# Gate and up tiles beside attention: three groups of eight pieces instead of two of twelve

## The chip, the core and the metric

The kernel runs on one core of a Trainium2 chip. The core has five engines, each with its own queue of instructions that it takes in order: PE (TensorE: matmuls, and their weight loads, PEld), DVE (VectorE), ACT (ScalarE), POOL (GpSimd) and SP (SyncE, which here only issues DMAs; POOL and ACT issue some too). They wait for each other through semaphores. The metric is the device time of one execution in microseconds (us).

## The reference

One transformer block with conditioning, in float32: S = 2048 rows, D = 512 columns, 32 heads of 16, a feed-forward part of F = 1792 columns. Six vectors (shift, scale and gate for each half) come from the condition `c`.

```python
mod = (_silu(c) @ w_mod).reshape(c.shape[0], 6, 1, -1)
sa, ca, ga, sb, cb, gb = (mod[:, i] for i in range(6))
h = _layernorm(x) * (1 + ca) + sa
qkv = split_heads(h @ wqkv)                    # 32 heads of 16
p = softmax(q @ k.T * 16 ** -0.5)              # whole rows, 2048 x 2048 per head
x = x + ga * (merge_heads(p @ v) @ wo)
h = _layernorm(x) * (1 + cb) + sb
x = x + gb * ((silu(h @ w_gate) * (h @ w_up)) @ w_down)
```

## The kernel before

**Tiling.** The 2048 rows are four chunks of 512 (`NC`, `CW`), the heads eight groups of four (`NG`). A *unit* is one chunk of queries with one group of heads, 32 units in all; chunk 0 is units 0 to 7, and so on. A unit has 16 *steps*, one for each 128 keys, so there are 512 steps. A step has four *slots* (`pair_of`, one for each head of the group): a score matmul (L569) that ACT turns into exponentials (L571), and one maximum matmul (L521) whose row maxima DVE takes (L523). The maxima are for a unit ahead: step i takes those of step i + 20, since the exponentials of a unit need all its row maxima first. When a unit's maxima are done, they are written as two extra rows into its query tile `qop`: by `max_rows` through PE, ACT and two DMAs of SP (L540, `qop<-mr`), or by `max_turned` through DVE and eight DMAs of SP (L560, `qop<-turned`). The score matmuls of that unit read those rows. P times V (L584, `pv_step`) follows a few steps behind, in halves.

**Two kinds of stretches.** `plain(steps)` runs steps with attention alone, in windows of three slots; scores take turns in three PSUM banks (4, 5, 6), maxima in four (0, 1, 2, 3). `filled(places, work)` runs eight slots (two steps) and after slot r takes `places[r]` pieces of other work; then the halves of P times V stand in a block. Scores then have two banks (4, 5), maxima three (0, 1, 2), and the other work sums into banks 3 and 6 (`FBANKS`). A *piece* is one step of `accumulate`: two matmuls of 64 rows, side by side on the two halves of the array. A gate and up tile (128 columns of F, `gate_up`) is 24 pieces: 12 with one assignment of halves to banks (`ph` 0), 12 with the other. A pair of `down` is 12 pieces, 6 and 6. Between the two assignments `down` calls `read_both`: ACT reads one element of each bank, so that PE's second half waits until the first is through. `gate_up` had no such read; its two assignments fell into two groups.

**Who is scheduled where.** For chunks 0, 1 and 2 the output projection and the feed-forward part run beside the attention of later units: from `STARTS[ci]` (steps 147, 275, 403) on come 8 filled steps for the output projection, 12 plain ones, then the chunk's jobs: 14 tiles of gate and up (f = 0 to 13) and 14 of down. Chunk 2 has `REST` = 24 further plain steps ahead of its jobs, and leaves `KEEP` = 7 jobs to the end. What remains up to the next chunk's start is plain: `plain(STARTS[ci] - done // 4)`. Chunk 3 runs after attention.

**What goes by the count of steps.** Work that is tied to attention is put off with `at(i, f)` and comes after step i, whatever runs beside it. When the last unit of a chunk closes, `begin` allocates the next chunk's x2 tile (512 rows of x, one buffer) and loads it (SP, L704), one step later SP loads wo (L709), then POOL loads the attention's output (`load_o`, L725) and splits it (`split_o`, L730 and L731). The old chunk's x2 is written out by POOL after the last `down` (L872), four DMAs.

Of the kernel before, what the change touches and what calls it, by code (L numbers as in the profile page):

```python
# [43 lines left out]
PTS = 13  # L44
FBANKS = (3, 6)
KEEP = 7
REST = 24
NORM = 9
STARTS = (147, 275, 403)
TWO = (0, 3, 2, 2, 2, 2, 1, 0)  # L50
DOWN = (0, 3, 3, 0, 3, 3, 0, 0)
ALONE = {TWO: (0, 4, 0, 4, 0, 4, 0, 0), DOWN: (0, 6, 0, 0, 0, 6, 0, 0)}


# [47 lines left out]
def block_kernel(ctx, tc, x, wqkv, wo, w_gate, w_up, w_down, c, w_mod, out):  # L102
# [526 lines left out]
    def tile_mid():  # L629
        return pf.tile([P, 2, CW], F32R, name="mid", tag="mid", bufs=3)  # L630

    def tmp(name):
        return pf.tile([P, CW], F32, name=name, tag="tmp", bufs=4)
# [56 lines left out]
    class Chunk:  # L690
        def __init__(self, ci, x2, oT, hT):
            self.ci, self.x2, self.oT, self.hT = ci, x2, oT, hT
            self.w, self.wd, self.mid, self.mv, self.nt = {}, {}, {}, None, []
            self.places, self.ahead, self.loaded = None, 1, set()
            self.jobs = [(gate_up, (0,)), (gate_up, (1,))]
            for m in range(NF // FG):
                if m:
                    self.jobs.append((gate_up, (2 * m + 1,)))
                if m + 1 < NF // FG:
                    self.jobs.append((gate_up, (2 * m + 2,)))  # L700
                self.jobs += [(down, (m, 0)), (down, (m, 2))]
# [74 lines left out]
    def accumulate(outs, lhs, rhs, nk, after, halves, by_k=False, trade=None):  # L776


        terms = [(k, a, b) for k in range(nk) for a, b in ((0, 0), (0, 1), (1, 0))]
        z = len(terms) - 1  # L780
        if halves:
            for ph in range(2):
                for j, (k, a, b) in enumerate(terms):
                    for e in (ph, 1 - ph):
                        rows = slice(64 * (ph ^ e), 64 * (ph ^ e) + 64)
                        nc.tensor.matmul(outs[e], lhs(e, a, k)[rows], rhs(b, k)[rows],  # L786
                                         start=(ph == 0 and j == 0), stop=(j == z and (ph == 1 or trade is not None)),
                                         skip_group_check=(ph == 1 and trade is not None))
                    if j == z:
                        (after if ph else trade or (lambda: None))()  # L790
                    yield
        else:
            order = [(e, j) for e in range(2) for j in range(z + 1)]
            for e, j in sorted(order, key=lambda o: o[1] // 3) if by_k else order:
                k, a, b = terms[j]
                nc.tensor.matmul(outs[e], lhs(e, a, k), rhs(b, k), start=(j == 0), stop=(j == z))  # L796
                if e == 1 and j == z:
                    after()
                yield
# [31 lines left out]
    def out_pair(ch, t0, outs, halves):  # L831
        return accumulate(outs, lambda e, a, k: ch.oT[a][:, k, (t0 + e) * P:(t0 + e + 1) * P],
                          lambda b, k: ch.wo[k // 2][:, b, k % 2, :], NK,
                          lambda: posts.append(lambda: add_o(ch, t0, outs, True)), halves)
# [7 lines left out]
    def gate_up(ch, f, outs, halves):  # L842
        ch.load_gu(f + ch.ahead)
        if f == 0:
            ch.load_wd(0)
        ch.mid[f] = mid = tile_mid()

        def after():
            th = tmp("th")
            nc.scalar.activation(th, outs[0], AF.Tanh, scale=0.5)  # L850

            def later():
                q = tmp("q")
                nc.vector.scalar_tensor_tensor(q, th, 1.0, outs[0], op0=ALU.add, op1=ALU.mult)  # L854
                m32 = tmp("m32")
                nc.vector.tensor_mul(m32, outs[1], q)  # L856
                slow = halves or (ch.ci, f) == (last - 1, NF - 2)
                (nc.gpsimd.tensor_copy if slow else nc.scalar.copy)(mid[:, 0, :], m32)  # L858
                (nc.gpsimd if slow else nc.vector).tensor_sub(mid[:, 1, :], m32, mid[:, 0, :].bitcast(F32))  # L859
            posts.append(later)  # L860

        w = ch.w.pop(f)
        return accumulate(outs, lambda e, a, k: w[:, 2 * e + a, k, :], lambda b, k: ch.hT[b][:, k, :], NK, after,
                          halves)

    def down(ch, m, t0, outs, halves):
        def later():
# [34 lines left out]
    def scaled(ch):  # L902
        ch.load_gu(0)
        ch.norm_scale(nc.gpsimd)
        ch.nt = [tile_mid().bitcast(F32) for _ in range(2)]
        for t in range(4):
            ch.normalize(t)
# [65 lines left out]
    halves = [(i, half) for i in range(n) for half in range(2)]  # L973
# [67 lines left out]
    def plain(steps, tails=()):  # L1041

        nonlocal four, bank, beside
        beside = False
        assert steps % WIN == 0 and done % 4 == 0
        four, bank = Turn(0, 3, 1, 2), Turn(4, 5, 6)
        for w in range(4 * steps // WIN):
            for _ in range(WIN):
                pair_of()
            if w < len(tails) and tails[w]:  # L1050
                tails[w](four())
            pvs((HALVES[(w - 2) % 4] if done > 8 else 0) + (w == 4 * steps // WIN - 1), True)
            turns_behind()
            end_steps()

    def filled(places, work):

        nonlocal four, bank, beside
        beside = True
        four, bank = three, Turn(4, 5)  # L1060
        if done >= 4 * n - 4 * (LEAD - 1):
            places, bank = ALONE.get(places, places), Turn(4, 5, 0, 1, 2)
        for r in range(len(places)):
            pair_of()
            take(work, places[r])
            if r % 4 == 3:
                end_steps()
        hook()
        pvs(6, False)
        turns_behind()  # L1070
# [14 lines left out]
    for ci in range(last):  # L1085
        plain(STARTS[ci] - done // 4)
        ch = chunks[ci]
        for t0 in (0, 2):
            work = out_pair(ch, t0, outs, True)
            filled(TWO, work)  # L1090
            filled(TWO, work)
        behind.append([4, lambda: scaled(ch)])
        tails = [lambda tp, k=k: ch.turned(tp, k) for k in range(NK)]
        plain(NORM, [None] * NORM + tails[:3])
        plain(WIN, tails[3:])
        if ci == last - 1:
            plain(REST)
        for _ in range(len(ch.jobs) - (KEEP if ci == last - 1 else 0)):
            job, args = ch.jobs.pop(0)
            if args == (NF // FG - 1, 0):  # L1100
                plain(WIN)
            work = job(ch, *args, outs, True)
            for places in (TWO, TWO) if job is gate_up else (DOWN,):
                filled(places, work)
    chunks[last - 1].load_gu(NF - 2)
    filled((0,) * 4, iter(()))
# [23 lines left out]
    ch, chp = chunks[last], chunks[last - 1]  # L1130
# [54 lines left out]
```

## Time and profile before

| | |
|---|---|
| Time, median of 3 runs | 1827.91 us (1827.7 to 1832.59) |
| Profiled execution, span | 1827.6 us |
| PE | 1818.3 us busy |
| DVE | 1523.2 us busy |
| ACT | 1255.7 us busy |
| POOL | 459.9 us busy |
| DMA | 267.63 MB, mean 146 GB/s |

The exponentials run from 169 us to 1664 us. A row of the costliest groups names line, engine, operation, output and inputs, the count, then busy us, mean ns of one, and the idle time of the engine ahead of it with what ended it. A row of the timeline begins with the start and the duration in us; "x2" at its end means two of the kind back to back. A row of a window gives the stretch, its length, busy us with the count in brackets, the granted clock of PE, the mean busy share of the DMA engines and what they moved in GB/s. Times of PE's matmuls overlap, so their starts are what counts.

### The profile page before, as it was taken

The numbers are of one execution on the slowest core, as the hardware profiler recorded it, in microseconds if no ns is written. First come the engines' busy times: TensorE is split into PE (matmuls) and PEld (weight loads), VectorE is DVE, ScalarE is ACT, GpSimd is POOL, SyncE is SP. The second block draws the span as 40 slices with busy tenths as digits, with TensorE's granted clock in tenths as the row PEclk, the third lists the DMA queues.
The fourth block names the chain that finished last, engine by engine and source line by source line (L and its number), as shares of the span: only waits on it lengthen the run. The fifth ranks groups of instructions, "written<-read, shape, count | busy, mean of one in ns | idle before, by whom it ended". The sixth has DMA issues, their size and how long they took to land.

```text
span 1827.6 us, 41072 instructions
## 1 busy us (share of the span) xinstructions
PE 1818.3 (99%) x16904; PEld 1199.7 (66%) x16904; DVE 1523.2 (83%) x2554; ACT 1255.7 (69%) x2434; POOL 459.9 (25%) x538
## 2 busy tenths in 40 slices
PE   9999999999999999999999999999999999999999
PEld 7876444444455777776565777776464577767887
DVE  5578999999999888889999888889999988821544
ACT  4223888888888776777888777777888877774211
POOL 3612544556223111111123111111113011130200
PEclk9999999999999999999999999999999999999999
DMA  9884876667845454453544554444643536333742
GB/s 306 288 225 143 202 195 178 178 167 200 206 81 125 103 123 142 114 148 71 144 110 107 139 125 119 124 115 91 160 79 57 119 89 162 130 119 120 276 167 110
DMA packets 80488, 267.63 MB, mean 146 GB/s; under 512 B 19604, under 2 KB 24212, under 8 KB 59620
## 3 DMA queue, kind: packets, MB, share of 16 engines
q1 hardware_dynamic: 61324, 179.71, 34.1%
q0 software_dynamic: 18288, 84.49, 19.4%
q8 instruction: 133, 2.18, 0.5%
q10 hardware_dynamic: 688, 0.80, 0.2%
q14 instruction: 55, 0.45, 0.1%
HBM read 201.85 MB, written 62.13 MB: 144 GB/s over the span
## 4 chain that ended last, share of the span: by engine, by line
PE 82%; DVE 14%; ACT 1%; DMA 1%; issue 0%; SPq 0%; DVEq 0%; ACTq 0%
PE bank L584 21%; PE bank L786 20%; PE bank L569 14%; DVE mx L523 14%; PE bank L521 11%; PE bank L211 7%; PE bank L796 7%; DMA wm_ab<-in_w_mod 1%; PE bank L770 0%; DMA kop<-o_dr 0%; PE bank L163 0%; DMA rb<-d_dr 0%; ACT sq L820 0%; PE bank L839 0%; DVE v_flat L870 0%
## 5 line engine op out<-in xcount | busy, mean ns | idle before, releaser
L523 DVE TENSOR_REDUCE mx<-bank 128x1 f32<-128x512 f32 x2048 | 1274.3, 686 | 108.3 <-PE bank L521 54.6
L569 PE MATMUL bank<-qop,kop 50*128 50x512 f32 x2048 | 728.6, 425 | 0.4 <-ACT pt__16523 L571 0.2
L521 PE MATMUL bank<-kop,qop 48*128 48x512 f32 x2048 | 725.1, 425 | 0.3
L569 PEld LDWEIGHTS bank<-qop,kop 50*128 50x128 f32 x2048 | 343.6, 184 | 167.9 <-issue 49.7
L521 PEld LDWEIGHTS bank<-kop,qop 48*128 48x128 f32 x2048 | 344.0, 185 | 107.0 <-DVE mx L523 62.3
L786 PE MATMUL bank<-act,wgu 64*128 64x512 f32 x1872 | 301.4, 392 | 0.0
L786 PEld LDWEIGHTS bank<-act,wgu 64*128 64x128 f32 x1872 | 197.1, 187 | 24.3
L611 POOL TENSOR_TENSOR on<-o,rb 128x512 f32<-128x512 f32 x31 | 39.8, 1285 | 506.3 <-DMA rb<-d_dr 358.9
L786 PE MATMUL bank<-wd,mid 64*128 64x512 f32 x912 | 134.1, 397 | 0.1
L858 POOL CAST mid<-m 128x512 fp32r<-128x512 f32 x40 | 24.3, 607 | 380.9 <-DVE m L856 180.2
L786 PEld LDWEIGHTS bank<-wd,mid 64*128 64x128 f32 x912 | 88.3, 186 | 15.5 <-ACT first L893 3.2
L211 PE MATMUL bank<-hT,wqs 128*128 128x512 f32 x384 | 94.4, 397 | 0.4 <-DVE wqs L351 0.4
L854 DVE SCALAR_TENSOR_TENSOR q<-th,bank 128x512 f32<-128x512 f32 x56 | 38.2, 683 | 54.3 <-ACT th L850 54.3
L211 PEld LDWEIGHTS bank<-hT,wqs 128*128 128x128 f32 x384 | 70.7, 188 | 18.8 <-issue 2.9
L850 ACT ACTIVATE th<-bank 128x512 f32<-128x512 f32 x56 | 33.3, 594 | 57.9 <-PE bank L796 57.9
L870 DVE TENSOR_TENSOR x<-bank,x 128x512 f32<-128x512 f32 x84 | 53.9, 685 | 19.0 <-PE bank L786 16.8
L856 DVE TENSOR_TENSOR m<-bank,q 128x512 f32<-128x512 f32 x56 | 38.7, 692 | 21.7 <-PE bank L796 19.7
L859 POOL TENSOR_TENSOR mid<-m,mid 128x512 fp32r<-128x512 f32 x40 | 51.6, 1289 | 3.3
L796 PE MATMUL bank<-wd,mid 128*128 128x512 f32 x216 | 51.5, 394 | 0.0
L211 PE MATMUL bank<-wqs,hT 128*128 128x512 f32 x192 | 48.1, 398 | 0.0
L786 PE MATMUL bank<-wgu,act 64*128 64x512 f32 x288 | 47.0, 393 | 0.0
L796 PEld LDWEIGHTS bank<-wd,mid 128*128 128x128 f32 x216 | 40.4, 188 | 9.0 <-POOL mid L859 0.2
(6301 smaller groups left out, 5148.9 us busy)
## 6 DMA issues: line engine op xcount, KB each, us to landing
wgu<-gu_dr SPq DMA_DIRECT2D x48, 1024.0 KB
wd<-wd_dr SPq DMA_DIRECT2D x28, 1024.0 KB
kop<-kd SPq DMA_DIRECT2D x33, 768.0 KB
kop<-kd POOLq DMA_DIRECT2D x29, 768.0 KB, 8.7
gu_dr<-wgu POOLq DMA_DIRECT2D x14, 1024.0 KB, 13.6
kd<-prt SPq DMA_DIRECT2D x16, 512.0 KB
qd<-prt SPq DMA_DIRECT2D x16, 512.0 KB
kop<-gu_dr SPq DMA_DIRECT2D x8, 1024.0 KB
```

The lines of the kernel that those rows point to most:

```text
L211: nc.tensor.matmul(pt, lhs(a, k), rhs(b, k), start=(n == 0), stop=(n == 3 * nk - 1))
L521: nc.tensor.matmul(pm, qop[u][rows, s, qt * P:(qt + 1) * P], kop[u % 3][rows, s, kc * CW:(kc + 1) * CW], start=True, stop=True)
L523: nc.vector.tensor_reduce(mx[u][:, b, s, qt, kc:kc + 1], pm, op=ALU.max, axis=AX.X)
L569: nc.tensor.matmul(sp, kop[u % 3][rows, h // 2, kt * P:(kt + 1) * P], qop[u][rows, h // 2, :], start=True, stop=True)
L584: nc.tensor.matmul(pv[u][32 * h:32 * h + 32, cols], v_flat[:, e0:e0 + 32], p_[h][:, cols], start=(kt == 0 and half == 0), stop=(kt == 15), ...
L611: mul.tensor_mul(on, o, rb)
L786: nc.tensor.matmul(outs[e], lhs(e, a, k)[rows], rhs(b, k)[rows], start=(ph == 0 and j == 0), stop=(j == z and (ph == 1 or trade is not None)),
L796: nc.tensor.matmul(outs[e], lhs(e, a, k), rhs(b, k), start=(j == 0), stop=(j == z))
L854: nc.vector.scalar_tensor_tensor(q, th, 1.0, outs[0], op0=ALU.add, op1=ALU.mult)
L856: nc.vector.tensor_mul(m32, outs[1], q)
L859: (nc.gpsimd if slow else nc.vector).tensor_sub(mid[:, 1, :], m32, mid[:, 0, :].bitcast(F32))
L870: nc.vector.tensor_add(ch.x2[:, t, :], outs[e], ch.x2[:, t, :])
```

## The change

The first nine gate and up tiles of chunks 0 and 1 and the first six of chunk 2, 24 in all, run in three groups of eight pieces (`THREE`) where they ran in two of twelve (`TWO`). Such a tile takes six steps, not four. The steps come out of plain stretches: of the 21 plain steps between chunk 0's jobs and chunk 1, and between chunk 1's and chunk 2, 18 go, and `REST` goes from 24 to 12. As the change of halves now falls into the middle group, these tiles call `read_both` too, with an empty slot behind it.

```diff
-REST = 24
+REST = 12
...
 TWO = (0, 3, 2, 2, 2, 2, 1, 0)
 DOWN = (0, 3, 3, 0, 3, 3, 0, 0)
+THREE = ((0, 2, 1, 1, 2, 1, 1, 0), (0, 2, 1, 1, 0, 2, 2, 0), (0, 2, 1, 1, 2, 1, 1, 0))
+SLOW = (9, 9, 6)
...
         return accumulate(outs, lambda e, a, k: w[:, 2 * e + a, k, :], lambda b, k: ch.hT[b][:, k, :], NK, after,
-                          halves)
+                          halves, trade=halves and f < SLOW[ch.ci] and read_both or None)
...
             work = job(ch, *args, outs, True)
-            for places in (TWO, TWO) if job is gate_up else (DOWN,):
+            for places in (DOWN,) if job is down else THREE if args[0] < SLOW[ci] else (TWO,) * 2:
                 filled(places, work)
```

The lines behind the first edit move by two (L704 becomes L706, and so on).

**A group of slots, on PE.** The last slots of chunk 0's first gate and up group, before (L569 is a score, L521 a maximum, L786 half a piece; `bank_67` and `bank_68` are the scores' two banks):

```order
L569 MATMUL bank_68<-qop,kop_971 128x512
L521 MATMUL bank_64<-kop_1509,qop 128x512
L786 MATMUL bank_66<-act_1609,wgu 128x512
L786 MATMUL bank_69<-act_1609,wgu 128x512
L786 MATMUL bank_66<-act_1610,wgu 128x512
L786 MATMUL bank_69<-act_1610,wgu 128x512
L521 MATMUL bank_65<-kop_1509,qop 128x512
L569 MATMUL bank_67<-qop,kop_971 128x512
```

The same group now, from its second slot on:

```order
L571 MATMUL bank_68<-qop,kop_971 128x512
L523 MATMUL bank_63<-kop_1509,qop 128x512
L788 MATMUL bank_66<-act_1609,wgu 128x512
L788 MATMUL bank_69<-act_1609,wgu 128x512
L788 MATMUL bank_66<-act_1610,wgu 128x512
L788 MATMUL bank_69<-act_1610,wgu 128x512
L523 MATMUL bank_64<-kop_1509,qop 128x512
L571 MATMUL bank_67<-qop,kop_971 128x512
L788 MATMUL bank_66<-act_1609,wgu 128x512
L788 MATMUL bank_69<-act_1609,wgu 128x512
L523 MATMUL bank_65<-kop_1509,qop 128x512
L571 MATMUL bank_68<-qop,kop_971 128x512
```

Where two pieces stood between slots, one or two stand now, so the scores of one bank come closer together.

**The end of chunk 0, on POOL.** Before, the four output DMAs of the old chunk (`out_0<-x2_1606`) stood ahead of everything of the next chunk (`on` is the attention's output times its reciprocal sums, `act0` and `act1` the next chunk's split output):

```order
L611 TENSOR_TENSOR on_10433<-o_9445,rb_10408 128x512
L612 DMA o_dr_81<-on_10433 128x512
L872 DMA out_0<-x2_1606 128x512 x4
L445 DMA kop0_88<-kd_79 48x2x2048
L445 DMA qop_10728<-qd_78 48x2x512
L611 TENSOR_TENSOR on_10891<-o_10159,rb_10864 128x512
L612 DMA o_dr_81<-on_10891 128x512
L725 DMA act1_10868<-o_dr_81 128x1x512 x4
```

Now they stand behind them, and behind the last tile's `mid`:

```order
L613 TENSOR_TENSOR on_10805<-o_9911,rb_10767 128x512
L614 DMA o_dr_81<-on_10805 128x512
L727 DMA act1_10771<-o_dr_81 128x1x512 x4
L860 CAST mid_10732<-m32_10900 128x512
L861 TENSOR_TENSOR mid_10732<-m32_10900,mid_10732 128x512
...
L732 CAST act0_10770<-act1_10771 128x512
L733 TENSOR_TENSOR act1_10771<-act1_10771,act0_10770 128x512
L874 DMA out_0<-x2_1606 128x512 x4
L447 DMA kop1_971<-kd_79 48x2x2048
```

What moved: the four output DMAs, from steps 251.5 and 253.5 to 269.5 and 271.5, and so from ahead of the next chunk's rows to behind them.

**The same place, on SP.** The order there is the same before and now: the reciprocal sums (`d_dr`, `rb`), the loads of x2 and wo, and unit 17's maxima (`mr`); now:

```order
L602 DMA d_dr_80<-dn_10552 128x16
L607 DMA rb_10767<-d_dr_80 128x1x512
L706 DMA x2_10769<-in_A_x 128x4x512
L711 DMA wgu_10808<-wo_dr_84 128x2048
L711 DMA wgu_10809<-wo_dr_84 128x2048
L541 DMA qop_9841<-mr_11192 2x8x128 x2
```

Nothing moved here against each other; but `x2_10769` takes the buffer of `x2_1606`, whose output DMAs moved as shown above, and the two rows of mr now come directly ahead of the first score that reads them (step 272), where they came two steps ahead of it.

## The prediction

> **What bounds the kernel now.** I read the page first (busy times and the costliest groups), then the maxima per stretch of time, then single rows of one group of slots, and last the queues at the end of a chunk's feed-forward part.
>
> ```profile
> PE 1818.3 (99%) x16904; PEld 1199.7 (66%) x16904; DVE 1523.2 (83%) x2554; ACT 1255.7 (69%) x2434; POOL 459.9 (25%) x538
> PE 82%; DVE 14%; ACT 1%; DMA 1%; issue 0%; SPq 0%; DVEq 0%; ACTq 0%
> L523 DVE TENSOR_REDUCE mx<-bank 128x1 f32<-128x512 f32 x2048 | 1274.3, 686 | 108.3 <-PE bank L521 54.6
> ```
>
> PE is booked as busy for the whole span (a waiting matmul counts), so this page alone can't tell who is late. DVE at 83% and PE's 82% of the chain say that they take turns. The maxima L523 are a clock: four are one attention step. Counted in five windows (busy us, and the count in brackets):
>
> ```profile
> 280.00:400.00 120.00, 119.41 (x200) 1.00 0.70 184
> 640.00:760.00 120.00, 90.60 (x141) 1.00 0.48 124
> 1020.00:1140.00 120.00, 91.79 (x143) 1.00 0.53 127
> 882.00:932.00 50.00, 49.86 (x84) 1.00 0.63 150
> 1285.00:1335.00 50.00, 49.76 (x84) 1.00 0.64 153
> ```
>
> In plain steps (first row) DVE is full: 200 maxima are 50 steps in 120 us, 2.40 us a step. Beside gate and up (second and third rows) maxima fill 76% of DVE and a step takes 120/35.25 = 3.40 us; there PE sets the pace. The last two rows are the plain steps between two chunks (step 254 to 275, and 382 to 403), 2.38 us each. So the change moves matmuls from a place where PE is the bound to one where PE has room. A group of twelve pieces, row by row on PE:
>
> ```profile
> 655.40 0.50 PE L521 MATMUL bank<-kop,qop 48*128 48x512 f32 x1
> 655.74 0.38 PE L569 MATMUL bank<-qop,kop 50*128 50x512 f32 x1
> 656.68 0.39 PE L569 MATMUL bank<-qop,kop 50*128 50x512 f32 x1
> 657.39 0.39 PE L569 MATMUL bank<-qop,kop 50*128 50x512 f32 x1
> 659.96 0.39 PE L569 MATMUL bank<-qop,kop 50*128 50x512 f32 x1
> 660.28 0.40 PE L584 MATMUL bank<-pt__7612,v_flat 128*32 128x256 f32 x1
> 662.15 0.49 PE L569 MATMUL bank<-qop,kop 50*128 50x512 f32 x1
> ```
>
> Slot 1 starts 0.34 us after slot 0. From slot 2 (656.68) to slot 7 (659.96) stand nine pieces and five slots: 3.28 us / 14 = 0.234 us for a slot's pair or a piece (each is two matmuls side by side). From slot 7 to the next group's slot 0 (the four halves of P times V) pass 2.19 us. A group of twelve is 0.34 + 18 x 0.234 + 2.2 = 6.75 us, and the measured 2 x 3.40 = 6.80: nothing but PE bounds it.
>
> **The change, part by part.** All sums are against the profiled execution, whose span is 1827.6 us; the median of the three runs shown is 1827.91, the same.
>
> Term 1, the groups. One tile and the two plain steps that go into it took 2 x 6.80 + 2 x 2.40 = 18.4 us. After, they are three groups of eight pieces. By PE alone a group is 0.34 + 14 x 0.234 + 2.2 = 5.82, three are 17.46: 0.94 less a tile, 24 x 0.94 = 22.6 us less in all. But the slots now come closer together, and in a filled group the scores have two banks only (4 and 5), where plain steps have three. What a bank needs to come round, on ACT (exponentials of the same group) and at one wait that PE itself shows:
>
> ```profile
> 655.93 0.60 ACT L571 ACTIVATE pt__7669<-bank 128x512 f32<-128x512 f32 x1 [1.16 <-PE bank L521]
> 656.43 0.59 ACT L571 ACTIVATE pt__7674<-bank 128x512 f32<-128x512 f32 x1
> 657.13 0.60 ACT L571 ACTIVATE pt__7687<-bank 128x512 f32<-128x512 f32 x1
> 657.83 0.60 ACT L571 ACTIVATE pt__7696<-bank 128x512 f32<-128x512 f32 x1
> 881.49 0.60 ACT L571 ACTIVATE pt__10624<-bank 128x512 f32<-128x512 f32 x1 [1.42 <-PE bank L569]
> 882.14 0.18 PEld L569 LDWEIGHTS bank<-qop,kop 50*128 50x128 f32 x1 [0.41 <-ACT pt__10624 L571]
> ```
>
> An exponential starts 0.53 us after the group's first score (655.40 to 655.93), 0.44 after a later one (657.39 to 657.83), or 0.50 after the one before it; it reads for 0.60, and the next score in its bank starts 0.05 later (881.49 + 0.60 to 882.14). Written out for 0, 2, 1, 1, 2, 1, 1, 0: slots start at 0, 0.34, 1.18 (PE would be there at 1.04), 1.68, 2.26 (2.15), 2.96, 3.43, 4.04 (3.90), and with 2.2 the group takes 6.24. The middle one (0, 2, 1, 1, 0, 2, 2, 0) waits at slots 4 and 5 and takes 6.36. The three maxima banks need 0.6 us a maximum and don't add to this. A tile is 18.84 then, 0.44 more than before, 10.6 us in all. So the ends are -22.6 and +10.6. I take **+6**: the bank rows are measured here and bind, and only their last hundredths are open.
>
> Edits at nothing: the 48 new tiny ACT reads between the two halves of a tile's sum. DOWN groups have them already, and the windows above, which hold such groups, show no slower step. Two slots stand on PE between the halves and cover them; without that cover PE would wait for up to one exponential that is ahead on ACT, 0.5 us, 12 us in 24 tiles. One unit of the third chunk takes its maxima out by DVE and eight small DMAs in place of PE and two: under half a us.
>
> Term 2, the end of chunks 0 and 1. Nine longer tiles push the last DOWN job from steps 250 to 254 to steps 268 to 272, but the next chunk's start stays by the count of steps: at step 262 SP gets the load of x2, at 263 the two loads of wo. x2 is one buffer, and its last readers are the four output DMAs of the old chunk, the last two now at 271.5. SP waits there, and behind it stand the two DMAs of unit 17's maxima (`qop<-mr`), without which the score at step 272 can't start. Before, those loads found x2 free:
>
> ```profile
> 878.79 1.29 DVE L870 TENSOR_TENSOR x<-bank,x 128x512 f32<-128x512 f32 x2
> 879.78 1.14 POOL L872 DMA_DIRECT2D out<-x  x2 [5.77 <-DVE x L870]
> 880.95 0.50 PE L569 MATMUL bank<-qop,kop 50*128 50x512 f32 x1
> out<-x POOLq DMA_DIRECT2D x4, 256.0 KB, 2.6
> 899.85 0.34 SPq L600 DMA_DIRECT2D d_dr<-dn  x1
> 903.11 0.57 SPq L605 DMA_DIRECT2D rb<-d_dr  x1
> 903.86 0.39 SPq L704 DMA_DIRECT2D x<-in_A_x  x1
> 904.30 1.11 SPq L709 DMA_DIRECT2D wgu<-wo_dr  x2
> 909.86 1.28 POOL L611 TENSOR_TENSOR on<-o,rb 128x512 f32<-128x512 f32 x1 [22.88 <-ACT pt__10974 L571]
> 926.22 1.28 POOL L731 TENSOR_TENSOR act<-act,act 128x512 fp32r<-128x512 f32 x1
> 919.10 1.12 SPq L539 DMA_DIRECT2D qop<-mr  x2
> ```
>
> The last DOWN's additions, its output DMAs and the first score after it are the rows from 878.79 to 880.95. The second of the two DMAs goes out at 880.4 and lands 2.6 us later, at 883.0: 2.0 us after the score would start. Then x2, wo and mr are issued, 2.7 us from the first row to the last (0.39 + 1.11 + 1.12 and gaps). A small DMA lands 3.3 us after its issue (899.85, whose landing 903.11 waits for), so PE would be held 2.0 + 2.7 + 3.3 = **8 us at least**. If the rows of mr queue behind the 3 MB, the transfer counts:
>
> ```profile
> 904.00:906.00 2.00, 0.00 (x0) 1.00 0.29 88
> 906.00:908.00 2.00, 0.00 (x0) 1.00 0.97 271
> 908.00:910.00 2.00, 0.00 (x0) 1.00 1.08 374
> 910.00:912.00 2.00, 0.00 (x0) 1.00 1.02 418
> 912.00:914.00 2.00, 0.00 (x0) 1.00 1.03 430
> ```
>
> At those GB/s (last column) 3.1 MB are through at 914, 10 us after x2's issue: 2 + 10 + between 1 and 3.3 for mr itself, 13 to **16 us at most**. I take 13, since all five DMAs go through one queue; with two such places (chunk 0 to 1 and 1 to 2) **+26**. While PE waits there, DVE and ACT have nothing either: the maxima stand behind the score on PE. Behind mr on SP nothing is due before step 273.5. POOL doesn't make it later: there the output DMAs now stand behind `on`, the loads of o and their splitting, 17.6 us from 909.86 to the end at 927.5. With rb issued near step 262.6 and `on` 6.8 us (two filled steps) later, that ends near step 270.6, before the last outputs are due at 271.5; if it were late, each us would add to the wait.
>
> The Trainium skill (DMA: Bandwidth & Descriptors, "Queues, rings and completion order") says that descriptors of one issuer's ring are consumed in ring order on each engine; by it mr comes behind wo and the dearer end holds, and no run here shows it yet. It also says (TensorE: Matmul & The Clock Gate, "What's actually happening") that PE's clock halves after an idle window of about 3.4 us; the granted clock is 1.00 in every window above, none of which has such a wait, and by an estimate from that page each of the two waits would cost about 1 us more.
>
> The sum: 1827.6 + 6 + 26 = 1859.6, so 1860.
>
> **Rivals.**
> - mr is not held by the 3 MB: 8 us a place, 1827.6 + 6 + 16 = 1850. For it: its two DMAs are small and could pass on idle engines; against it, the DMAs are at 97% and more from 906 on.
> - The slots reach PE's pace: 1827.6 - 23 + 26 = 1831, no measurable difference (about 0.3%, 5.5 us, is what a measurement of this kernel tells from none). For it: PE is the bound of every filled group now. Against it: slots 0.47 us apart, where a bank takes 0.44 + 0.60 + 0.05 = 1.09 for two.
> - The other side: PE's freed room is gained whole and the boundary costs its least, 1827.6 - 23 + 16 = 1821. It takes both at once; it decides when the gain of 24 tiles passes both waits by 5.5 us, that is, with a wait of 8.5 us or less at 0.94 us a tile.
> - The wait isn't there, because POOL's outputs or SP's loads come otherwise than I read them: with my groups 1834, just slower.
>
> **How the numbers follow.** Forecast 0.72, the first rival 0.08, PE's pace 0.10, the other side 0.04, no wait 0.03, dearer than my ends 0.03. The range takes the forecast and the first rival: 8 us a place and -6 from the groups is 1838, 16 a place and +12 is 1872. Slower by over 0.3%: 0.72 + 0.08 + 0.03 + 0.03 = 0.86; faster 0.04; within it 0.10.
>
> **What would show it.** The groups: the 24 maxima of a tile in 18.6 us or so, and PE's loads L571 waiting for exponentials; at 17.5 us with none, term 1 is wrong. The boundary: after step 272 a gap of about 13 us on DVE at two places, SP's x2 issue right behind a landing of an output DMA, and mr's two DMAs 1.6 us later; a gap of 8 means mr passed the loads, none means that I read the queue wrong. A gap of another kind, above all at slot 0 of a tile for the banks 3 and 6 that DVE still reads, would be a cost I left out.

## The result and the profile after

The changed kernel takes 1900.03 us (median of four runs, 1898.51 to 1901.84), the kernel before 1828.33 beside it: a ratio of 1.0386, with a 95% interval of 1.0370 to 1.0402. The forecast of 1860 had the sign and both places right; the time lies 28 us above the range. The profiled execution has a span of 1896.8 us, 69.2 more than before. Lines of the code stand two further down: scores L571, exponentials L573, maxima L523 and L525.

The page of the kernel after, in the order of before's (busy times, chain by engine, costliest groups):

```profile
PE 1854.6 (98%) x16898; PEld 1189.1 (63%) x16898; DVE 1517.2 (80%) x2556; ACT 1258.5 (66%) x2481; POOL 460.4 (24%) x538
...
PE 93%; DVE 2%; DMA 2%; ACT 1%; SPq 0%; issue 0%; POOL 0%; DVEq 0%
...
L525 DVE TENSOR_REDUCE mx<-bank 128x1 f32<-128x512 f32 x2048 | 1268.7, 681 | 185.3 <-PE bank L523 131.8
L571 PE MATMUL bank<-qop,kop 50*128 50x512 f32 x2048 | 761.8, 435 | 34.2 <-DMA qop<-mr 34.0
```

DVE does the same work and idles 77 us more ahead of its maxima (185.3 against 108.3), and its share of the chain fell from 14% to 2%. It has become the engine that waits. The last row names one new wait, 34.0 us for the DMA that carries row maxima. The rest has no such row and lies inside the groups. The scores of one group (places 0, 2, 1, 1, 2, 1, 1, 0) on PE (start, duration), with the next group's first at the end:

```profile
659.23 0.49 PE L571 MATMUL bank<-qop,kop 50*128 50x512 f32 x1
...
659.57 0.38 PE L571 MATMUL bank<-qop,kop 50*128 50x512 f32 x1
...
660.41 0.50 PE L571 MATMUL bank<-qop,kop 50*128 50x512 f32 x1
...
660.99 0.41 PE L571 MATMUL bank<-qop,kop 50*128 50x512 f32 x1
...
661.59 0.50 PE L571 MATMUL bank<-qop,kop 50*128 50x512 f32 x1
661.60 0.49 PE L523 MATMUL bank<-kop,qop 48*128 48x512 f32 x1
661.93 0.63 PE L788 MATMUL bank<-act,wgu 64*128 64x512 f32 x4
662.40 0.39 PE L523 MATMUL bank<-kop,qop 48*128 48x512 f32 x1
662.40 0.39 PE L571 MATMUL bank<-qop,kop 50*128 50x512 f32 x1
...
663.48 0.49 PE L571 MATMUL bank<-qop,kop 50*128 50x512 f32 x1
665.77 0.50 PE L571 MATMUL bank<-qop,kop 50*128 50x512 f32 x1
```

and the exponentials of its slots 0 and 2 on ACT:

```profile
659.76 0.60 ACT L573 ACTIVATE pt__7680<-bank 128x512 f32<-128x512 f32 x1 [1.41 <-PE bank L523]
...
660.94 0.60 ACT L573 ACTIVATE pt__7704<-bank 128x512 f32<-128x512 f32 x1
```

Slots 0, 2 and 4 share a bank. Slot 0 starts at 659.23, its exponential 0.53 later and reads for 0.60, and 0.05 after that slot 2 starts (660.41): 1.18 us. From slot 2 to slot 4 (661.59) it is 1.18 again, by the same three parts. The group takes 6.54 us, the other two of the tile 6.56 and 6.61: 19.7, where two groups and two plain steps took 18.4. So 24 tiles cost 24 x 1.3 = 31 us.

The other place is the end of chunk 0, on POOL and then on SP (the bracket holds the idle time before a row and what ended it):

```profile
934.05 1.14 POOL L874 DMA_DIRECT2D out<-x  x2 [5.75 <-DVE x L872]
935.18 0.59 POOL L447 DMA_DIRECT2D kop<-kd  x1
935.90 0.58 POOL L447 DMA_DIRECT2D qop<-qd  x1
```

```profile
937.30 0.38 SPq L706 DMA_DIRECT2D x<-in_A_x  x1
937.73 1.04 SPq L711 DMA_DIRECT2D wgu<-wo_dr  x2
938.87 1.14 SPq L541 DMA_DIRECT2D qop<-mr  x2
```

DVE's first maxima after it and after the end of chunk 1, and PE's first scores after the first of the two:

```profile
953.49 3.68 DVE L525 TENSOR_REDUCE mx<-bank 128x1 f32<-128x512 f32 x6 [17.94 <-PE bank L523]
1389.47 3.08 DVE L525 TENSOR_REDUCE mx<-bank 128x1 f32<-128x512 f32 x5 [18.04 <-PE bank L523]
```

```profile
952.65 0.76 PE L571 MATMUL bank<-qop,kop 50*128 50x512 f32 x1 [16.93 <-DMA qop<-mr]
952.65 0.79 PE L523 MATMUL bank<-kop,qop 48*128 48x512 f32 x1
953.22 0.62 PE L571 MATMUL bank<-qop,kop 50*128 50x512 f32 x1
```

The windows there, and below them three from the end of chunk 1, where PE's first score starts at 1388.64 (the last three columns are PE's granted clock, the mean busy share of the DMA engines, GB/s):

```profile
940.00:944.00 4.00, 0.00 (x0) 0.00 (x0) 0.00 (x0) 0.00 (x0) 0.00 (x0) 0.50 0.93 126
944.00:948.00 4.00, 0.00 (x0) 0.00 (x0) 0.00 (x0) 0.00 (x0) 0.00 (x0) 0.50 1.06 394
948.00:952.00 4.00, 0.00 (x0) 0.00 (x0) 0.00 (x0) 0.00 (x0) 0.00 (x0) 0.50 0.86 361
952.00:956.00 4.00, 3.35 (x16) 2.28 (x20) 2.52 (x5) 2.55 (x6) 0.00 (x0) 0.50 0.03 6
956.00:960.00 4.00, 4.00 (x34) 1.66 (x31) 2.66 (x5) 2.56 (x6) 0.00 (x0) 0.53 0.02 2
960.00:964.00 4.00, 3.88 (x43) 2.00 (x37) 2.76 (x5) 2.73 (x6) 0.00 (x0) 1.00 0.99 166
...
1390.00:1392.00 2.00, 2.00 (x12) 1.06 (x13) 2.00 (x5) 2.00 (x6) 0.00 (x0) 0.50 0.00 0
1392.00:1394.00 2.00, 2.00 (x20) 0.88 (x14) 1.15 (x2) 0.87 (x3) 0.00 (x0) 0.69 0.00 0
1394.00:1396.00 2.00, 2.00 (x26) 0.92 (x23) 1.95 (x4) 1.78 (x5) 0.00 (x0) 1.00 0.09 16
```

Two things are to be seen. SP's order is the one foretold: x2 goes out as the output DMAs land (937.17 in the trace), then wo, then mr. But two loads of POOL (`kop`, `qop` of unit 19, 960 KB) went out 2 us ahead of x2, and in their stretch the DMA engines are 93% busy and move 126 GB/s. They land at 944.0 and 945.0, and only then does the x2 and wo traffic run at 394 GB/s. And when PE starts again it has the clock at 0.50, until 956 and beyond; scores of one stretch, 0.34 us apart in a normal group, start 0.57 apart (952.65 to 953.22).

By steps (from exponential to exponential), 268 to 275 took 41.2 us and 396 to 403 took 39.9. The normal length, two groups of before and three plain steps, is 2 x 6.80 + 7.2 = 20.8. So the two ends cost 20.4 and 19.1, together 39.5. With the 31 of the groups that is 70.5. From the first exponential to the last the two executions differ by 70.7, and their spans by 69.2.

### The profile page after: what moved, and what is told of

It reads as the page before. It is cut to its first block, busy times and chain, and to the rows that moved or that the text cites. A ratio compares the mean times of both kernels' runs of the same rounds, so it can differ in the third digit from the quotient of the medians.

```text
span 1896.8 us, 41114 instructions
## 1 busy us (share of the span) xinstructions
PE 1854.6 (98%) x16898; PEld 1189.1 (63%) x16898; DVE 1517.2 (80%) x2556; ACT 1258.5 (66%) x2481; POOL 460.4 (24%) x538
## 4 chain that ended last, share of the span: by engine, by line
PE 93%; DVE 2%; DMA 2%; ACT 1%; SPq 0%; issue 0%; POOL 0%; DVEq 0%
PE bank L586 25%; PE bank L571 20%; PE bank L788 19%; PE bank L523 13%; PE bank L798 7%; PE bank L213 7%; DVE mx L525 2%; DMA qop<-mr 1%; PE bank L841 1%; DMA wm_ab<-in_w_mod 0%; PE bank L772 0%; PE bank L165 0%; DMA out<-x 0%; ACT sq L822 0%; PE bank L537 0%
## 5 line engine op out<-in xcount | busy, mean ns | idle before, releaser
L525 DVE TENSOR_REDUCE mx<-bank 128x1 f32<-128x512 f32 x2048 | 1268.7, 681 | 185.3 <-PE bank L523 131.8
L571 PE MATMUL bank<-qop,kop 50*128 50x512 f32 x2048 | 761.8, 435 | 34.2 <-DMA qop<-mr 34.0
L523 PE MATMUL bank<-kop,qop 48*128 48x512 f32 x2048 | 744.2, 428 | 0.4
L571 PEld LDWEIGHTS bank<-qop,kop 50*128 50x128 f32 x2048 | 345.9, 185 | 264.5 <-issue 93.3
L523 PEld LDWEIGHTS bank<-kop,qop 48*128 48x128 f32 x2048 | 346.6, 185 | 93.9 <-DVE mx L525 50.4
L788 PE MATMUL bank<-act,wgu 64*128 64x512 f32 x1872 | 342.4, 394 | 0.0
L788 PEld LDWEIGHTS bank<-act,wgu 64*128 64x128 f32 x1872 | 202.9, 186 | 23.6 <-DVE m L858 1.1
L613 POOL TENSOR_TENSOR on<-o,rb 128x512 f32<-128x512 f32 x31 | 39.9, 1286 | 452.4 <-DMA rb<-d_dr 412.4
L858 DVE TENSOR_TENSOR m<-bank,q 128x512 f32<-128x512 f32 x56 | 38.7, 692 | 21.7 <-PE bank L798 19.7
L447 POOL DMA_DIRECT2D kop<-kd x29 | 16.9, 582 | 132.1 <-PE bank L788 115.8
```

Source lines behind the costliest of these rows:

```text
L523: nc.tensor.matmul(pm, qop[u][rows, s, qt * P:(qt + 1) * P], kop[u % 3][rows, s, kc * CW:(kc + 1) * CW], start=True, stop=True)
L525: nc.vector.tensor_reduce(mx[u][:, b, s, qt, kc:kc + 1], pm, op=ALU.max, axis=AX.X)
L571: nc.tensor.matmul(sp, kop[u % 3][rows, h // 2, kt * P:(kt + 1) * P], qop[u][rows, h // 2, :], start=True, stop=True)
L613: mul.tensor_mul(on, o, rb)
```

## The experiments

The first five ask how the loss divides and what holds a group; the next four take the chunk ends apart; the last three shorten the groups.

**1. Groups without the chunk ends** (from the changed kernel).

```diff
-SLOW = (9, 9, 6)
+SLOW = (0, 0, 6)
```

> Only chunk 2's six tiles run in three groups; chunks 0 and 1 are as before, so no chunk ends late. Theory G (a three-group tile costs 19.7 us as the trace of the changed kernel shows, against 18.4 before): 6 x 1.3 = +8 us, 1836. Rival (the groups cost what I forecast, 18.65, and all the rest of the loss is made at the ends of chunks 0 and 1): +1.5 us, 1829.

Measured: 1838.1 us, ratio 1.0049 (1.0034 to 1.0064), 8.9 us above the kernel before beside it. Most of its groups take 6.53 to 6.58 us (two take 6.64 and 6.68), and there is no gap. So a tile costs about 1.5 us by this time, and the groups alone are slower than what they replace, as the theory has it.

**2. The chunk end without the groups** (from the kernel before).

```diff
         plain(WIN, tails[3:])
+        if ci < last - 1:
+            plain(18)
```

> No tile in three groups; 18 plain steps of chunks 0 and 1 are moved ahead of their jobs, so that the last DOWN ends at steps 272 and 400 as in the changed kernel. Theory G: two waits of 18 us and a slow restart of 1 to 2 us each, +38 to +40 us, 1867. Rival of my record (13 us each): +26, 1854. If the long wait needs the three-group tiles ahead of it, less than 20.

Measured: 1885.23 us, 1.0308 (1.0293 to 1.0324), 56 us more, against an expected 39. The waits on PE, in us, times and longest:

```profile
PE bank L569 <- DMA qop<-mr: 34.3, 2, 17.3
PE bank L786 <- DMA wgu<-gu_dr: 9.6, 2, 5.1
```

The first row and the steps 268 to 275 and 396 to 403 (40.7 and 40.1 us) give back the boundary of the changed kernel: 39 us without one group of eight. The second row is another wait, for gate weights, at steps 229 and 357: groups of 14.33 and 12.86 us in place of 6.75. The two make 13.7 us, 9.6 of it the wait itself. The changed kernel has no such wait, so it comes with the shift of the 18 plain steps. Some 3 us of the 56 stay without a row.

**3 and 4. Empty groups with two and with three score banks** (from the kernel before; the 24 plain steps ahead of chunk 2's jobs as filled groups with no pieces; the second one gives those groups plain steps' banks, three for scores and four for maxima).

```diff
-            plain(REST)
+            for _ in range(REST // 2):
+                filled((0,) * 8, iter(()))
```

> The kernel before, with chunk 2's 24 REST plain steps run as twelve filled groups without any piece. Theory (the two score banks and the block of P times V bound a group from below): slots at 0, 0.34, 1.18, 1.68, 2.27, 2.77, 3.36, 3.86 and 2.3 us behind, 6.15 us a group against 4.8 for two plain steps, 12 x 1.35 = +16 us, 1844. Rival (a group costs only its PE work or DVE's eight maxima, whichever is more: 4.8 us): no change.

```diff
-    def filled(places, work):
+    def filled(places, work, *turns):
...
-        four, bank = three, Turn(4, 5)
+        four, bank = turns or (three, Turn(4, 5))
...
-            plain(REST)
+            for _ in range(REST // 2):
+                filled((0,) * 8, iter(()), Turn(0, 1, 2, 3), Turn(4, 5, 6))
```

> As the empty groups, with three score banks and four maxima banks (banks 3 and 6 are idle there). Theory: ACT's and DVE's pitch then bound the slots, the last at 3.2 us, 5.5 us a group, +8 us, 1836. Rival (banks don't matter, the loss is the block of P times V alone): the same as the empty groups with five banks.

Measured: 1865.29 us, 1.0199 (1.0183 to 1.0214), for the first, and 1839.18, 1.0056 (1.0040 to 1.0073), for the second. The scores of an empty group with two banks:

```profile
1401.71 0.39 PE L569 MATMUL bank<-qop,kop 50*128 50x512 f32 x1
...
1402.55 0.50 PE L569 MATMUL bank<-qop,kop 50*128 50x512 f32 x1 [0.21 <-ACT pt__17357 L571]
...
1403.73 0.49 PE L569 MATMUL bank<-qop,kop 50*128 50x512 f32 x1 [0.19 <-ACT pt__17369 L571]
```

Every second score waits for an exponential, and slots 2 and 4 are 1.18 us apart with nothing between them: such a group starts at 1401.37 and takes 6.33 us, to 1407.70. The expectation had 6.15. With the banks of plain steps the same eight slots take 5.43 (1440.66 to 1446.09). Run 4 has a third score bank and a fourth maxima bank at once; that it is the scores' bank that counts is read from the rows above, whose waits end with an exponential. So the score banks hold an eight-slot group at 6.33 even when it is empty, against 4.80 for two plain steps: 0.90 us go with the banks, and 0.63 stay without them. The first run lost 36 us and not the 18 that these groups give, for another reason. In its windows, with the granted clock third from the end:

```profile
1405.00:1410.00 5.00, 4.63 (x43) 2.36 (x43) 3.55 (x7) 3.12 (x7) 1.86 (x2) 1.00 0.16 56
1410.00:1415.00 5.00, 4.94 (x32) 2.46 (x36) 3.66 (x9) 2.79 (x7) 0.00 (x0) 0.60 0.00 0
1415.00:1420.00 5.00, 4.81 (x24) 2.51 (x17) 2.64 (x5) 2.36 (x5) 0.00 (x0) 0.50 0.02 3
```

Where the clock is halved, its groups take 7.6 to 8.7 us. The fourth run has the clock at 0.998 over its span, but it fell in two of the twelve groups there too: they take 7.20 and 7.04, 3.4 us more than two at 5.43. The first of the two:

```profile
1420.00:1425.00 5.00, 5.00 (x42) 2.26 (x42) 2.83 (x6) 2.31 (x6) 0.29 (x1) 0.66 0.98 160
```

**5. Other places for the pieces** (from 1, six tiles).

```diff
-THREE = ((0, 2, 1, 1, 2, 1, 1, 0), (0, 2, 1, 1, 0, 2, 2, 0), (0, 2, 1, 1, 2, 1, 1, 0))
+THREE = ((0, 2, 1, 1, 1, 1, 1, 1), (0, 2, 1, 1, 0, 2, 1, 1), (0, 2, 1, 1, 1, 1, 1, 1))
```

> Chunk 2 only, with the pieces at 0, 2, 1, 1, 1, 1, 1, 1 (middle group 0, 2, 1, 1, 0, 2, 1, 1), one piece less ahead of slots 5 and 6 and one behind slot 7. Theory (a score that waits for its bank also loses its partner and the early weight load, so PE falls behind by more than the wait): with the pieces nearer to the score banks' own rhythm a group takes 6.3 to 6.4 us, not 6.54: 1838 - 3 = 1835. Rival (the place of the pieces doesn't matter): 1838.

Measured: 1837.51 us, 1.0049 (1.0034 to 1.0064): no change from 1. The groups take 6.57. Slot 5 comes earlier (2.87 us after slot 0, for 3.17), but slots 2 and 4 come at 1.19 and 2.37 as before, so the banks' 1.18 for two slots stays, and the piece behind slot 7 stands ahead of the P times V block. Spreading isn't the lever.

**6. x2 behind mr** (from the changed kernel, all 24 tiles).

```diff
-        ch.load_x2(nc.sync if ci else nc.gpsimd)
+        if not ci:
+            ch.load_x2(nc.gpsimd)
...
+                at(i + 15, lambda: chunks[u // NG].load_x2(nc.sync))
```

> The changed kernel, but the loads of the next chunk's x2 are issued behind unit 17's and unit 25's maxima (mr) on SP, not ahead of them. Theory: the 18 us gap at steps 272 and 400 was mr behind x2's wait and the 3 MB; without it PE waits only for mr's own way (PE, ACT, two DMAs, some 4 to 5 us), and PE's slow restart goes too: 1900 - 2 x 15 = 1870. Rival (what holds mr is POOL's load of unit 19's keys on the same DMA engines, landed 9 us after the last score): a gap of 9 to 10 us, 1881.

Measured: 1884.62 us, 1.0308 (1.0293 to 1.0324), 15 us back of 39, nearer the rival. mr goes out at 935.94 and DVE still idles:

```profile
945.81 3.68 DVE L525 TENSOR_REDUCE mx<-bank 128x1 f32<-128x512 f32 x6 [10.37 <-PE bank L523]
```

The first score starts at 944.98, right behind POOL's loads of unit 19 (landed 943.9 and 944.5). Two DMAs of 8 KB wait for 960 KB of another queue.

**7 and 8. The loaders apart.** The first is 6 with mr made one group (two steps) earlier, so that it goes out (929.82) ahead of POOL's loads of unit 19 (936.73) as well. The second is the changed kernel with unit 19 and 27 loaded through SP's queue, behind mr.

```diff
+                if ci < last - 1:
+                    for b in behind:
+                        b[0] = 1
```

> As the one before, and mr is made one group (two steps) earlier. Theory: no gap is left at steps 272 and 400, only the groups' loss of 24 x 1.3 = 31 us: 1860. Rival (x2 and wo now arrive too late for the next chunk, or a wait of another kind takes the place): 1865 or more, with a wait elsewhere between steps 270 and 283.

```diff
-        load_parts(kop[u % 3], kd, u % NG, 0, S, nc.gpsimd if u > 2 else nc.sync)
+        load_parts(kop[u % 3], kd, u % NG, 0, S, nc.gpsimd if u > 2 and u not in (19, 27) else nc.sync)
...
+        if u in (19, 27):
+            second = first = nc.sync
```

> The changed kernel, but the keys and queries of units 19 and 27 are loaded by SP alone, behind mr; POOL loads none of them. Theory: POOL's load took the DMA engines from 935 to 945 us, ahead of x2 and wo, and made 13 us into 18: two gaps of 13, 1900 - 10 = 1890. Rival (the 3 MB alone take 18 us): no change, 1900.

Measured: 1862.93 us, 1.0190 (1.0175 to 1.0205), for the first: no gap is left, steps 268 to 275 take 22 us, and what remains is the groups' 31 and some 3 us. 1889.16, 1.0335 (1.0317 to 1.0352), for the second; its gap is the 13 us that the prediction took:

```profile
948.88 3.68 DVE L527 TENSOR_REDUCE mx<-bank 128x1 f32<-128x512 f32 x6 [13.29 <-PE bank L525]
```

So the predicted 13 is what x2 and wo ahead of mr cost, and POOL's loads are the 5 us on top. Run 7 took mr out of the way of both at once.

**9. Both at once** (6 with the edit of 8).

> The changed kernel with x2 behind mr, and with the keys and queries of units 19 and 27 on SP alone, behind mr too: nothing else is on the DMA engines when mr is issued. Theory (with x2 alone put behind, the gap of 10.6 us ended when POOL's load had landed, at 944 to 945 us): now mr's own way is left, 4 to 5 us, 1885 - 12 = 1873. Rival (mr takes 10 us by itself): no change, 1885.

Measured: 1878.32 us, 1.0262 (1.0232 to 1.0291).

```profile
939.32 3.68 DVE L527 TENSOR_REDUCE mx<-bank 128x1 f32<-128x512 f32 x6 [3.76 <-PE bank L525]
```

The gap is 3.76 as the theory has it, and steps 268 to 272 take 17.6 and 17.0. The time missed its 1873 by 5, and the steps 275 to 283 and 403 to 423 took 4.2 us each more than in the changed kernel. x2 goes out at 947.41 there, behind the loads that moved onto SP, and the trace names it as what is waited for. DVE's first addition to x2:

```profile
963.93 1.29 DVE L812 TENSOR_TENSOR x<-bank,x 128x512 f32<-128x512 f32 x2 [2.88 <-DMA x<-in_A_x]
```

PE's next pieces wait for that addition in turn. No run moves x2 alone.

**10 to 12. Shorter groups.** Two of the four halves of P times V in a group move behind slot 3, where PE would otherwise wait for a score bank: six tiles (from 1), then 24 on top of 7, then with the tile's first pieces later.

```diff
-THREE = ((0, 2, 1, 1, 2, 1, 1, 0), (0, 2, 1, 1, 0, 2, 2, 0), (0, 2, 1, 1, 2, 1, 1, 0))
+THREE = ((0, 3, 1, 0, 0, 3, 1, 0),) * 3
...
+            if r == 3 and places in THREE:
+                pvs(2, False)
```

> Chunk 2's six tiles in three groups of eight as before in this study, but P times V stands in two blocks (two halves behind slot 3, two behind slot 7), with the pieces at 0, 3, 1, 0, 0, 3, 1, 0. Theory (what holds a group at 6.55 us is the round of the two score banks, 1.18 us for two slots with nothing on PE to fill it): the blocks give the exponentials time, no score waits, and PE alone sets 16 x 0.234 + 8 x 0.216 + 2 x 0.34 = 6.15 to 6.2 us a group, although PE has one more change of work: 18 x 0.37 = 7 us less than with one block, 1831. Rival (the pieces or the ACT reads cost it): no change or slower, 1838 or more.

> All 24 tiles in three groups, with P times V in two blocks, x2 behind mr, and mr a group earlier. Theory: both costs are away, 24 tiles of 18.5 us against 18.4: 1829 to 1833, within half a per cent of the kernel before. Rival (a cost I haven't named remains): over 1840.

Measured: 1834.77 us, 1.0032 (1.0016 to 1.0049), and 1857.32, 1.0145 (1.0119 to 1.0171). Most groups now take 6.19 to 6.21 as foretold, but the first run missed its 1831 by 4, and the second is 24 to 28 us over its 1829 to 1833. Both expectations were wrong in taking every group to be like that. The first group of one tile in two, on PE and on DVE:

```profile
1466.46 0.50 PE L571 MATMUL bank<-qop,kop 50*128 50x512 f32 x1
...
1467.06 0.50 PE L788 MATMUL bank<-act,wgu 64*128 64x512 f32 x1
1467.85 0.73 PE L788 MATMUL bank<-act,wgu 64*128 64x512 f32 x4 [0.30 <-DVE m L858]
...
1468.65 0.39 PE L571 MATMUL bank<-qop,kop 50*128 50x512 f32 x1
```

```profile
1466.33 0.68 DVE L856 SCALAR_TENSOR_TENSOR q<-th,bank 128x512 f32<-128x512 f32 x1
1467.11 0.69 DVE L858 TENSOR_TENSOR m<-bank,q 128x512 f32<-128x512 f32 x1
```

The tile's first pieces want banks 3 and 6, and DVE's `q` and `m` of the tile before read them until 1467.80. The group shown takes 7.08 (those of chunks 0 and 1 mostly 7.01), and the first down group of a pair 7.63 where it took 6.83. Over two tiles and their down groups (starts of exponentials): 39.40 to 38.12 for the six groups, 13.74 to 14.55 for the down groups, so 0.47 less, 5.6 in twelve such pairs. Against the kernel before beside each, run 7 lost 34.7 and this one 28.1: 6.6 apart.

```diff
-THREE = ((0, 3, 1, 0, 0, 3, 1, 0),) * 3
+THREE = ((0, 0, 3, 1, 0, 3, 1, 0),) + ((0, 3, 1, 0, 0, 3, 1, 0),) * 2
```

> The kernel with both losses undone as far as tried (1857.32), with the first four pieces of each tile's first group moved behind slot 2 and slot 3 (0, 0, 3, 1, 0, 3, 1, 0; the two later groups stay 0, 3, 1, 0, 0, 3, 1, 0). The maths is that of the changed kernel. Theory: what was left there is the tile's first piece, which wants banks 3 and 6 while DVE's q and m of the tile before still read them; in the run with P x V in two, m ends 1.33 us after the group's slot 0 (1442.65 to 1443.98) and the first piece starts 1.39 after it, where PE stood from 0.65 on. With slots 0 to 2 ahead of it PE works until 1.3 to 1.4, so the first group takes 6.4 to 6.5 us in place of 7.0, 0.5 to 0.6 a tile: 1843 to 1846 us, and the waits of L788 for DVE's m (24 of them) go. Rival: the wait is not on the path, since the maxima behind m on DVE are late by as much whatever PE does; then slot 3 waits for its maxima bank instead and it stays at 1855 or more.

Measured: 1862.21 us, 1.0182 (1.0165 to 1.0199), 33.6 above the kernel before beside it, where the version without the edit was 28.1 above. The waits of pieces for `m` fell from 24 to 11, and the late group from 7.01 to 6.87, but the first group of the other tile rose from 6.20 to 6.87. Its row on PE says why:

```profile
1451.72 0.49 PE L571 MATMUL bank<-qop,kop 50*128 50x512 f32 x1 [0.19 <-ACT pt__17702 L573]
1451.72 1.19 PE L788 MATMUL bank<-act,wgu 64*128 64x512 f32 x6
```

Slot 2 now waits for its score bank with no pieces ahead of it (1450.54 to 1451.72, 1.18 again), and the pieces come behind the wait. The rival's time came, but by the score bank, not by the maxima bank that it named. No version here beats the kernel before.

## Why the prediction was wrong

**The bound: right.** PE set the pace of filled groups and the plain steps had room. That DVE's share of the chain fell to 2% agrees.

**Term 1, the groups: right mechanism, wrong size** (+6 foretold, about +31 measured). The prediction had the two score banks as what binds. Run 3 shows their round of 1.18 us with nothing else on PE, and run 10, which fills the pauses with P times V at the same two banks, has groups of 6.20. Two steps in it fell. First, "0.44 after a later one" and "0.234 us for a slot's pair or a piece" were read in a full group of twelve. A score that had to wait for its bank has its exponential 0.53 later and the next piece 0.34 later (661.59 to 661.93). So slot 4 comes at 2.36 for 2.26 and slot 5 at 3.17 for 2.96; with 2.29 from slot 7 to the next group (663.48 to 665.77) for 2.2 the group is 6.54 for 6.24. Second, "I take **+6**" lay below the 10.6 that the same count gave, and no row spoke for a value under the count. The first is worth 24 x 0.87 = 21 us, the second 4.6. Run 5 shows that a more even spread of the pieces would not have saved it.

**Term 2, the chunk ends: right mechanism, wrong size** (+26 foretold, 39.5 measured). The wait, its two places and SP's order came as written, and so did its cause as far as x2 and wo go. Run 2 shows the loss without the groups, run 7 its end with neither x2 nor POOL's loads ahead of mr. What failed is the upper end, "13 to **16 us at most**": it counted 3 MB from x2's issue at the rate of before's windows, and left out that POOL issues unit 19's loads at the same step. They came out 2 us ahead of x2. The order of POOL's instructions, shown ahead of the prediction, has the first of them as its last row (`kop1_971<-kd_79`), right behind the output DMAs that the prediction did count. Runs 6, 8 and 9 put prices on the loaders: a gap of 13.3 with x2 and wo alone, 10.4 with unit 19 alone, 3.8 with neither, 17.9 with both. The two gaps, 17.94 and 18.04, are 10 us over the 26. The second omission is the restart at half clock. It was in no term. The rows show the clock at 0.50 to 0.53 from the restart at 952.65 until 960, and from 1388.64 until between 1392 and 1394 at the second end. The steps there cost 2.5 and 1.1 us more than the gaps; the clock is the reason that the rows show, and the end with the longer half clock lost more, though no run separates it. Beside the sum stood an estimate of about 1 us a place, from the Trainium skill (TensorE: Matmul & The Clock Gate, "What's actually happening"); the second end agrees with it, the first took more.

**The edits put at nothing: not contradicted.** The read between a tile's halves stands in the tile's middle group, which takes 6.56 us, between the other two (6.54 and 6.61); foretold were 6.36 and 6.24.

**The rivals.** "mr is not held by the 3 MB" fell (run 8: 13.3 us with nothing but the 3 MB in the way). "The slots reach PE's pace" and "the other side" fell with the bank rows. The range reached to +12 and 16 a place; both terms went past it in the same direction.

## What to carry to other kernels

A lag between two engines that was measured where the first had not waited is too short for a place where it has: count a buffer's whole round from a row in which that wait stands, and where a hand count comes out at a value, don't forecast a cheaper one without a row that speaks for it. Before a loop is made lighter by spreading it over more turns, find what a turn costs when it is empty (6.33 us here against 4.80 for the steps given up), since each added turn pays that. When work that goes by its own progress is shifted against work that goes by a step count, list the DMAs of every queue that falls due at that step, not of the waiting queue alone.

## What the runs showed of the hardware

The granted clock of PE was 0.50 after both waits of 17 us in the changed kernel. It was back at 1.00 about 7 us after the first restart (952.65; 0.53 in 956 to 960) and about 4.6 us after the second (1388.64; 0.69 in 1392 to 1394). The Trainium skill (TensorE: Matmul & The Clock Gate, "What's actually happening") gives about 3.4 us of sustained work to return to full clock; both restarts took longer, the first about twice that. A fall came with a far shorter wait, too: in run 9 PE stood for 2.8 us and restarted at 938.48, and the granted clock was 0.51 from 938 to 940 and 0.50 up to 944.

In run 3 the clock fell to 0.50 (1415 to 1420 us) with matmuls in every window and no long gap; by the trace PE only waited 0.2 us at every second score. The Trainium skill (TensorE: Matmul & The Clock Gate, "A second HAM failure mode: psum-queue depth-cycling") describes a clock that falls and rises again and again from many short pauses, and run 3 agrees. The same scores, maxima and P times V take 4.80 us in two plain steps, 5.43 in a group of run 4 and 6.33 in one of run 3. The clock stays at 1.00 in the first, fell twice in the second and again and again in the third. Run 4's trace shows no wait of PE over 0.14 us there, so whether the waits or the little work per us brings the clock down is not shown. The changed kernel's groups, with pieces in the pauses, showed none of it.

Two DMAs of 8 KB took until 944.98 when POOL's 960 KB had been issued just before (run 6), and the gap shrank from 10.37 to 3.76 us when those loads stood behind them (run 9).
